# Whole 128-row products in place of packed 64-row halves for the filling work of an attention and Fourier-mixing kernel

## The chip, the cores and the metric

The kernel runs on one core of one Trainium2 chip. The metric is device time in microseconds (us) of one execution. The kernel before took 1701.76 us as the median of two runs (1701.06 to 1702.46).

## The reference

A token matrix `x` of 2048 x 512 goes through softmax attention with 32 heads of 16 columns, and another matrix through a two-sided Fourier product. A gate per token mixes the two:

```
q, k, v = split(x @ wqkv);  a = softmax(q k^T / 4) v @ wo          # 32 heads, 2048 x 2048 scores each
a2 = Bx @ Wd_re^T;  b2 = Bx @ Wd_im^T                               # 2048 x 512
b = Ws_re @ a2 - Ws_im @ b2                                         # 2048 x 2048 times 2048 x 512
g = sigmoid(sum(x * gate_w));  out = g * a + (1 - g) * b
```

The Fourier matrices come in as plain data. All operands are fp32. Products that must be exact to more than one rounded operand are made as three products of rounded parts: high by high, high by low, low by high.

## The kernel before, in words

**Stages.** A first part, up to about 600 us, makes q, k, v and both hidden-side Fourier products and most of the sequence-side product, and scans the scores for row maxima beside it. The second part is a loop of 512 steps, one per head pair `p` (16), half of the queries `h` (2) and block of 128 keys `kb` (16). A step makes scores (`qk`, line 232, operands `qs` and `ks` with 50 rows per head), takes their exponentials on ACT (`qk_both` and `qk_single`, lines 256 and 264) and adds values times exponentials (`pv`, line 825) into one PSUM bank `pvb`.

**Kinds of products.** TensorE's array has 128 rows. Three shapes of product meet in the loop:

- Score products take 50 rows, one head on rows 0 to 49 and the other on rows 64 to 113, so two of them run as a pair, one in each half of the rows. Their operands are fp32r (fp32 rounded for a single pass).
- Products of values take all 128 rows and 17 columns; four of them stand side by side in the columns (`tile_position=(0, r)`, with r in 0, 32, 64, 96). Their operands are fp32, and each shows as two records.
- Fourier and output products go through `halves_of` (line 203): the 128 rows of a product are cut into two products of 64 rows and 128 columns in fp32r, which run as a pair and write two PSUM banks `ps[0]` and `ps[1]`. Whoever reads the result adds the two banks.

**Filling.** Up to step 316 the loop also scans scores for the maxima of later pairs (line 157). From step `MIX` = 317 on no scan is left, and `outputs()` fills the steps instead: a generator, of which each step takes one piece by `next(fill)`. It runs through

- `spectral(t)` for two blocks of Fourier rows (one piece of 3 products per step, 16 steps each),
- `crosses()`: 14 groups of 24 products, 3 per step, over steps 349 to 460; `gather` (line 1099) reads each finished group, a copy of bank 0 and an addition of bank 1,
- from step `OUT` = 461 `mix_heads(t, steps)` for 16 blocks of output rows, 9 products each in two pieces of 4 and 5 (or four pieces of 2, 2, 2 and 3 for t = 0, 2 and 4); `take_in` (line 940) adds bank 0 and then bank 1 into the output tile `ys[t]`,
- `mix_some(t, (0, 1))` for six pairs of output blocks, one piece of 3 products per step and block group, by `mix_rest`.

Every group writes `pair_banks()`, a pair of PSUM banks of which there is one copy. The next group's first product waits until the readers of the group before have ended.

**What sets the order.** Nothing reorders the engines' queues: instructions run in the order in which Python writes them. In an even step the piece of filling comes first, then the scores; in an odd step it comes after the scores. Products of values of two steps are made together in the even steps, after the scores. So a period of two steps reads on TensorE: scores, products of values, scores, filling of the odd step and of the next even step.

Of the kernel before, what the change touches and what calls it, by code (L numbers as in the profile page):

```python
# [24 lines left out]
NB = S // P  # L25
# [25 lines left out]
MIX = TOTAL - FRONT + 1  # L51
OUT = MIX + NB * LATER - SAVED
# [16 lines left out]
def build(tc, xT, xr, wqkv, wo, wrT, wiT, cr, ci, ct, gate, out):  # L69
    nc = tc.nc  # L70
    with ExitStack() as ctx:
# [131 lines left out]
        def halves_of(ps, lhs, rhs, first, last):  # L203

            for j in range(2):
                r = slice(64 * j, 64 * j + 64)
                nc.tensor.matmul(ps[j], lhs[r], rhs[r], start=first, stop=last)  # L207

        def block(i):
            return big.tile([P, 512], F32R, tag=f"b{i}", name=f"b{i}")  # L210
# [62 lines left out]
        with ExitStack() as pf:  # L273
# [150 lines left out]
            with ExitStack() as px:  # L424
# [247 lines left out]
                for t in range(NB):  # L672
                    if 0 <= t - 2 < NB - 4:
                        after(32, split_operand, t - 2, load_operand(0, t - 2, rp), nc.gpsimd)
                    if t == 8:
                        first = stk.tile([P, 4, CS, P], F32, tag="stk", name="first")
# [10 lines left out]
            with ExitStack() as py:  # L687
# [38 lines left out]
                for n, (ph, t, u) in enumerate(coef):  # L726
# [41 lines left out]
                    for w in range(CS):  # L768
                        s = u * CS + w
# [9 lines left out]
                    if u == NU - 1:  # L779
                        tx = cp.tile([P, D], F32, tag="tx", name="tx")  # L780
                        last = n == len(coef) - 1
# [18 lines left out]
        with ExitStack() as pa:  # L800
# [63 lines left out]
            ys, oc = {}, {}  # L864
# [74 lines left out]
            def take_in(t, ps):  # L939
                nc.vector.scalar_tensor_tensor(ys[t], ps, g[:, t:t + 1], ys[t], op0=ALU.mult, op1=ALU.add)  # L940
# [20 lines left out]
            def spectral(t):  # L961

                ps = pair_banks()
                y = ap.tile([P, D], F32, tag="take", name="y", bufs=3)
                nc.sync.dma_start(y, y_d[t // 4][:, t % 4, :])
                for s in range(NB):
                    if s % CS == 0:
                        hi, lo = parts.pop(0)
                        load_unit()
                    if s % CS == 1:  # L970
                        split_unit()
                    w = s % CS
                    for i, (c_, a_) in enumerate(((hi, ah[s]), (hi, al[s]), (lo, ah[s]))):
                        halves_of((ps[:, 0, :], ps[:, 1, :]), c_[:, w, :], a_, s == 0 and i == 0, s == NB - 1 and i == 2)
                    if s < NB - 1:
                        yield
                for j in range(2):
                    nc.vector.scalar_tensor_tensor(y, ps[:, j, :], gm[:, t:t + 1], y, op0=ALU.mult, op1=ALU.add)
                nc.sync.dma_start(y_d[t // 4][:, t % 4, :], y)
                yield  # L980
# [117 lines left out]
            def gather(n, f, ps, r):  # L1098

                t = place(28 + f if n == 0 else 30 + f if n == 1 else None)  # L1100
                nc.vector.tensor_copy(t, ps[:, 0, :])
                nc.vector.tensor_add(t, ps[:, 1, :], t)
                add, sub = nc.gpsimd.tensor_add, nc.gpsimd.tensor_sub
                if n < 2:
                    tiles["nw"[n], f] = t
                if n == 1:
                    x = place()
                    add(x, tiles["n", f], t)
                    finish(r, (0, 1), f, x)
                elif n == 2:  # L1110
                    tiles["x", f] = t
                    sub(tiles["w", f], tiles["w", f], t)
                elif n == 3:
                    x = tiles["x", f]
                    add(x, x, t)
                    finish(r, (1, 0), f, x)
                    sub(tiles["n", f], tiles["n", f], t)
                elif n == 4:
                    sub(tiles["n", f], tiles["n", f], t)
                elif n == 5:  # L1120
                    sub(tiles["n", f], t, tiles["n", f])
                    finish(r, (0, 0), f, tiles["n", f])
                    add(tiles["w", f], tiles["w", f], t)
                elif n == 6:
                    add(tiles["w", f], tiles["w", f], t)
                    finish(r, (1, 1), f, tiles["w", f])

            def crosses():

                for n in range(len(CROSSES)):  # L1130
                    for f in range(2):
                        ps = pair_banks()
                        for u in range(8):
                            left, right = sets[f, u // CS], sets[None, u]
                            q = slice((u % CS) * P, (u % CS + 1) * P)
                            for i, (a, b) in enumerate(((0, 0), (0, 1), (1, 0))):
                                halves_of((ps[:, 0, :], ps[:, 1, :]), left[a][:, q], right[b],
                                          u == 0 and i == 0, u == 7 and i == 2)
                            if u < 7:
                                yield  # L1140
                        gather(n, f, ps, now[0] - HALVED)
                        yield
# [11 lines left out]
            def mix_heads(t, steps):  # L1154

                q = slice((t % 4) * P, (t % 4 + 1) * P)
                ps = pair_banks()
                n, last, ends = 0, 3 * (ND - 1), [sum(steps[:i + 1]) for i in range(len(steps))]
                assert ends[-1] == last
                for f in range(ND - 1):  # L1160
                    for a, b in ((0, 0), (0, 1), (1, 0)):
                        halves_of((ps[:, 0, :], ps[:, 1, :]), oc[t // 4, f, a][:, q], w2[f][b], n == 0, n == last - 1)
                        n += 1
                        if n in ends[:-1]:
                            yield
                for j in range(2):
                    take_in(t, ps[:, j, :])
                yield

            def mix_rest(t, ps, k, first, last):  # L1170
# [73 lines left out]
            for step in range(NP * PERIODS):  # L1244
                p, i = step // PERIODS, step % PERIODS
                h, kb = i // NB, i % NB
                now[0] = step
                if i == 18:
                    rows = load_use(p + 1, step >= MIX)
                if i >= 18:  # L1250
                    next(rows, None)
                if step in (MIX - 24, MIX - 20):
                    load_unit()
                if step in (MIX - 9, MIX - 7):
                    split_unit(int(step > MIX - 9))
                if OUT - 10 <= step < OUT - 4 or step >= OUT + 4:
                    next(operands, None)
                if step in (OUT - 8, OUT + 1):
                    output_rows(int(step > OUT))
                for n, at in enumerate((OUT - 25, (NP - 1) * PERIODS)):  # L1260
                    if at <= step < at + 8:
                        load_y(8 * n + step - at)
                if step >= MIX and step % 2 == 0:
                    next(fill)
                if step == 0:
                    pend.append((p, h, kb, ahead[:2]))
                    continue
                es = ahead[2:] if step == 1 else [qk2(p, h, kb, 0)]
                if step == 1:
                    es.append(qk2(p, h, kb, 1))  # L1270
                    flush()
                if late:
                    late.pop(0)()
                if step == 2:
                    es.append(qk2(p, h, kb, 1))
                if step > 1:
                    next_scan()
                if step > 2:
                    es.append(qk2(p, h, kb, 1))
                if step >= MIX and step % 2:  # L1280
                    next(fill)
                if step == NP * PERIODS - 1:
                    part(3, 0)
                done = None
                for _ in range(min(len(pend), 1) if step < MIX else 0 if step % 2 else 2):
                    done = flush()
                if done and done[2] == NB - 1:
                    halved.append((step + (10 if done[0] < NP - 2 else 7 if done[0] < NP - 1 else 3), quotients(*done[:2])))
                if halved and halved[0][0] <= step:
                    p_, h_ = halved[0][1][:2]  # L1290
                    divide(*halved.pop(0)[1])
                    if p_ == NP - 2:
                        output_rest(h_)
                    if p_ == NP - 2 + (h_ == 0):
                        output_last(h_)
                pend.append((p, h, kb, es))
                sum_quarters(step)
                crossing(step - HALVED)
                if TURNED <= step < TURNED + CROSS:
                    load_turned(NB - CROSS + step - TURNED)  # L1300
                if TURNED + 11 <= step < TURNED + 11 + CROSS:
                    take_turned(NB - CROSS + step - TURNED - 11)
# [77 lines left out]
```

## Time and profile before

| what | value |
|---|---|
| median of the runs | 1701.76 us |
| profiled execution | 1701.12 us |
| its span in the profile | 1699.3 us |
| TensorE (PE) busy | 1687.0 us, 13524 matmul records |
| weight loads (PEld) busy | 1039.9 us |
| ACT busy | 1491.1 us |
| DVE busy | 1185.7 us |
| POOL busy | 817.5 us |

The profiled execution took 1701.12 us, 1.8 us more than its span. PE and PEld are two rows of TensorE: the products and the loads of their stationary operands. A load that starts while a product still runs costs nothing by itself. A "busy" PE includes the time in which a product's results still leave the array, so that the starts of products tell more than their durations.

### The profile page before, as it was taken

To read this page: it belongs to the slowest core of one execution; us is meant where nothing else is said; L and a number is where in the kernel's file an instruction comes from. 1 tells how busy PE (TensorE), PEld (TensorE's weight loads), DVE (VectorE), ACT (ScalarE), POOL (GpSimd) and SP (SyncE) were. 2 spreads that over 40 slices of the span, in tenths; PEclk is the share of its full clock that TensorE was granted. 3 is DMA by queue.
4 is the path that set the end of the run, shared out by engine and by line. 5 is a ranking of instruction groups with operands and counts; after the bars stand their busy time and mean duration, and the time that the engine had idled before them with its cause. 6 is when DMAs were issued, how large, how long until landed. Compare 5 with 4: busy or idle time off the path is not lost.

```text
span 1699.3 us, 34660 instructions
## 1 busy us (share of the span) xinstructions
PE 1687.0 (99%) x13524; PEld 1039.9 (61%) x13524; DVE 1185.7 (70%) x1528; ACT 1491.1 (88%) x2468; POOL 817.5 (48%) x997
## 2 busy tenths in 40 slices
PE   9999999999999999999999999999999999999998
PEld 7889988999998784333333333333345555555554
DVE  5798888999989996666666676766733456563343
ACT  6447889888888888999999999999998888888886
POOL 4676876655556760444555364453323233334222
PEclk9999999999999999999999999999999999999999
DMA  7784668544448763455445455453526565575833
GB/s 274 265 270 99 218 217 241 153 129 122 120 125 210 207 133 71 122 128 123 134 119 133 101 130 137 96 144 56 111 56 147 148 148 146 136 192 135 196 92 128
DMA packets 151572, 251.08 MB, mean 148 GB/s; under 512 B 49792, under 2 KB 60528, under 8 KB 144112
## 3 DMA queue, kind: packets, MB, share of 16 engines
q1 hardware_dynamic: 136144, 227.49, 49.4%
q0 software_dynamic: 14688, 20.33, 5.1%
q8 instruction: 106, 1.74, 0.5%
q10 hardware_dynamic: 576, 1.05, 0.2%
q14 instruction: 58, 0.48, 0.1%
HBM read 168.56 MB, written 81.01 MB: 147 GB/s over the span
## 4 chain that ended last, share of the span: by engine, by line
PE 89%; DMA 4%; DVE 3%; POOL 2%; issue 1%; SPq 0%; ACT 0%; DVEq 0%; POOLq 0%; ACTq 0%
PE pvb L825 29%; PE xy L207 21%; PE s L232 19%; PE s L207 8%; PE s L178 8%; PE s L157 5%; DVE mx L159 3%; DMA qs<-q_d 1%; DMA early<-b_d 1%; DMA q_d<-eh 0%; DMA craw<-cr 0%; DMA raws<-xT 0%; POOL s L320 0%; DMA raws<-wqkv 0%; DMA abr<-b_d 0%
## 5 line engine op out<-in xcount | busy, mean ns | idle before, releaser
L256 ACT ACTIVATE eb<-s 128x1024 f32<-128x1024 f32 x512 | 582.5, 1138 | 58.1 <-PE s L232 58.1
L264 ACT ACTIVATE e<-s 128x512 f32<-128x512 f32 x1022 | 613.0, 716 | 0.0
L159 DVE TENSOR_REDUCE mx<-s 128x2 f32<-128x1024 f32 x380 | 461.5, 1225 | 193.1 <-PE s L157 192.7
L825 PE MATMUL pvb<-eb,va 128*17 128x512 f32 x2052 | 514.4, 597 | 0.3 <-DVE ob L834 0.3
L825 PE MATMUL pvb<-e,va 128*17 128x512 f32 x2044 | 513.5, 597 | 0.0
L183 DVE TENSOR_REDUCE mx<-s 128x1 f32<-128x512 f32 x644 | 434.6, 690 | 45.9 <-PE s L178 37.7
L232 PEld LDWEIGHTS s<-qs,ks 50*128 50x128 f32 x2048 | 215.7, 184 | 362.4 <-ACT eb L256 268.8
L181 ACT ACTIVATE s<-s 128x512 f32<-128x512 f32 x644 | 373.3, 586 | 72.8 <-PE s L178 42.4
L232 PE MATMUL s<-qs,ks 50*128 50x512 f32 x2048 | 424.6, 436 | 0.1
L207 PE MATMUL xy<-b,c 64*128 64x512 f32 x2448 | 395.1, 391 | 0.6 <-DVE s L320 0.3
L178 PE MATMUL s<-ks,qs 64*128 64x512 f32 x1288 | 305.5, 392 | 1.2 <-DVE mx L159 0.5
L207 PEld LDWEIGHTS xy<-b,c 64*128 64x128 f32 x2448 | 288.1, 184 | 22.7 <-DVE s L320 0.9
L825 PEld LDWEIGHTS pvb<-eb,va 128*17 128x17 f32 x2052 | 69.8, 96 | 187.9 <-issue 178.1
L178 PEld LDWEIGHTS s<-ks,qs 64*128 64x128 f32 x1288 | 165.4, 184 | 19.8 <-DVE mx L183 3.1
L157 PE MATMUL s<-ks,qs 48*128 48x512 f32 x760 | 166.6, 394 | 0.0
L844 POOL DMA_DIRECT2D r_d<-lc x31 | 18.0, 580 | 267.8 <-DVE lc L843 220.0
L207 PE MATMUL s<-b,b 64*128 64x512 f32 x1050 | 136.1, 390 | 0.4 <-DMA b<-o_d 0.4
L408 POOL TENSOR_TENSOR c<-craw,c 128x512 fp32r<-128x512 f32 x84 | 108.6, 1293 | 14.6 <-DVE c L407 8.0
L207 PE MATMUL xy<-w,b 64*128 64x512 f32 x768 | 115.3, 391 | 0.0
L837 POOL DMA_DIRECT2D lc<-ob x124 | 63.1, 515 | 108.0 <-DVE ob L834 103.9
L207 PEld LDWEIGHTS s<-b,b 64*128 64x128 f32 x1050 | 99.6, 185 | 24.0 <-issue 1.0
L846 POOL DMA_DIRECT2D rb<-r_d x124 | 60.5, 495 | 101.9 <-DMA r_d<-lc 97.9
(147 smaller groups left out, 1570.0 us busy)
## 6 DMA issues: line engine op xcount, KB each, us to landing
qs<-q_d SPq DMA_DIRECT2D x90, 256.0 KB
craw<-cr SPq DMA_DIRECT2D x60, 256.0 KB
craw<-ct SPq DMA_DIRECT2D x48, 256.0 KB
ks<-k_d SPq DMA_DIRECT2D x46, 256.0 KB
ks<-kf_d SPq DMA_DIRECT2D x44, 256.0 KB
kept_None<-sum SPq DMA_DIRECT2D x40, 256.0 KB
craw<-kept_None SPq DMA_DIRECT2D x40, 256.0 KB
craw<-ci SPq DMA_DIRECT2D x32, 256.0 KB
```

Source lines behind the costliest of these rows:

```text
L157: nc.tensor.matmul(ps[:, j, :], qs[b:b + 48, qb * P:(qb + 1) * P], ks[b:b + 48, c * 512:(c + 1) * 512], start=True, stop=True)
L159: nc.vector.tensor_reduce(mx[p][:, :, qb, c], ps, axis=AX.X, op=ALU.max)
L178: nc.tensor.matmul(ps, qs[b:b + 64, qb * P:(qb + 1) * P], ks[b:b + 64, c * 512:(c + 1) * 512], start=first, stop=True, skip_group_check=True)
L181: nc.scalar.activation(ps, ps, AF.Relu)
L183: nc.vector.tensor_reduce(mx[p][:, j, qb, c // 2:c // 2 + 1], ps, axis=AX.X, op=ALU.max)
L207: nc.tensor.matmul(ps[j], lhs[r], rhs[r], start=first, stop=last)
L232: nc.tensor.matmul(pss[j], ks[b:b + 50, kb * P:(kb + 1) * P], qs[b:b + 50, q0:q0 + 512], start=True, stop=True)
L256: nc.scalar.activation(e, ps, AF.Exp, scale=SCALE)
L264: nc.scalar.activation(e[j], pss[j], AF.Exp, scale=SCALE)
L408: sub(lo, raw, hi.bitcast(F32))
L825: nc.tensor.matmul(pvb[r:r + VC, :], va[:, kb, 2 * p + j, :], es[c][j], start=kb == 0, stop=kb == NB - 1, tile_position=(0, r))
L837: nc.gpsimd.dma_start(lc[32 * n:32 * n + 32, :], ob[r + DH:r + VC, :].rearrange("p (s e) -> p s e", e=16))
```

## The change

A second helper `whole_of` makes one product of 128 rows into one bank. The places that use it are `spectral`, `crosses` and `mix_heads`; their readers lose the addition of the second bank. `mix_some` and the last pieces keep `halves_of`. From step `OUT` on, the even step's piece of filling is taken after the products of values instead of before the scores; odd steps stay as they were.

```diff
+        def whole_of(ps, lhs, rhs, first, last):
+
+            nc.tensor.matmul(ps, lhs, rhs, start=first, stop=last)
+
@@ spectral @@
-                        halves_of((ps[:, 0, :], ps[:, 1, :]), c_[:, w, :], a_, s == 0 and i == 0, s == NB - 1 and i == 2)
+                        whole_of(ps[:, 0, :], c_[:, w, :], a_, s == 0 and i == 0, s == NB - 1 and i == 2)
...
-                for j in range(2):
+                for j in range(1):
                     nc.vector.scalar_tensor_tensor(y, ps[:, j, :], gm[:, t:t + 1], y, op0=ALU.mult, op1=ALU.add)
@@ gather @@
                 nc.vector.tensor_copy(t, ps[:, 0, :])
-                nc.vector.tensor_add(t, ps[:, 1, :], t)
@@ crosses @@
-                                halves_of((ps[:, 0, :], ps[:, 1, :]), left[a][:, q], right[b],
-                                          u == 0 and i == 0, u == 7 and i == 2)
+                                whole_of(ps[:, 0, :], left[a][:, q], right[b],
+                                         u == 0 and i == 0, u == 7 and i == 2)
@@ mix_heads @@
-                        halves_of((ps[:, 0, :], ps[:, 1, :]), oc[t // 4, f, a][:, q], w2[f][b], n == 0, n == last - 1)
+                        whole_of(ps[:, 0, :], oc[t // 4, f, a][:, q], w2[f][b], n == 0, n == last - 1)
...
-                for j in range(2):
-                    take_in(t, ps[:, j, :])
+                take_in(t, ps[:, 0, :])
@@ the loop of steps @@
-                if step >= MIX and step % 2 == 0:
+                if MIX <= step < OUT and step % 2 == 0:
                     next(fill)
...
                     if p_ == NP - 2 + (h_ == 0):
                         output_last(h_)
+                if step >= OUT and step % 2 == 0:
+                    next(fill)
                 pend.append((p, h, kb, es))
```

The order of TensorE's queue in a step pair of `crosses()`, before (score products L232, halves of a filling product L207, written `x2`):

```order
L232 MATMUL s_17896<-qs,ks 128x512 x2
L232 MATMUL s_17900<-qs,ks 128x512
L232 MATMUL s_17901<-qs,ks 128x512
L207 MATMUL s_17744<-b_17629,b_17730 128x512 x2
L207 MATMUL s_17744<-b_17630,b_17730 128x512 x2
L207 MATMUL s_17744<-b_17629,b_17731 128x512 x2
L207 MATMUL s_17744<-b_17651,b_17730 128x512 x2
L207 MATMUL s_17744<-b_17652,b_17730 128x512 x2
L207 MATMUL s_17744<-b_17651,b_17731 128x512 x2
L232 MATMUL s_17925<-qs,ks 128x512 x2
L232 MATMUL s_17929<-qs,ks 128x512
L232 MATMUL s_17930<-qs,ks 128x512
```

and now (score products L236, whole products L211):

```order
L236 MATMUL s_17755<-qs,ks 128x512 x2
L236 MATMUL s_17759<-qs,ks 128x512
L236 MATMUL s_17760<-qs,ks 128x512
L211 MATMUL s_17621<-b_17519,b_17607 128x512
L211 MATMUL s_17621<-b_17520,b_17607 128x512
L211 MATMUL s_17621<-b_17519,b_17608 128x512
L211 MATMUL s_17621<-b_17538,b_17607 128x512
L211 MATMUL s_17621<-b_17539,b_17607 128x512
L211 MATMUL s_17621<-b_17538,b_17608 128x512
L236 MATMUL s_17777<-qs,ks 128x512 x2
L236 MATMUL s_17781<-qs,ks 128x512
L236 MATMUL s_17782<-qs,ks 128x512
```

Six pairs of halves became six single products in the same place; the chunk still stands between two groups of scores.

The same queue in the output part, before: the end of the products of values (L825), the scores of the odd step, and the start of a group of `mix_heads`, nine pairs of which follow one another.

```order
L825 MATMUL pvb<-eb,va 17x512 x2
L825 MATMUL pvb<-e_0_9973,va 17x512
L825 MATMUL pvb<-e_0_9976,va 17x512
L232 MATMUL s_21183<-qs,ks 128x512 x2
L232 MATMUL s_21187<-qs,ks 128x512
L232 MATMUL s_21188<-qs,ks 128x512
L207 MATMUL s_21205<-b_20311,b_20924 128x512 x2
L207 MATMUL s_21205<-b_20312,b_20924 128x512 x2
L207 MATMUL s_21205<-b_20311,b_20926 128x512 x2
```

And now (products of values L829): the five whole products that end a group stand behind the products of values, and the next group begins after one set of scores.

```order
L829 MATMUL pvb<-e_0_9976,va 17x512
L211 MATMUL s_20620<-b_19900,b_20149 128x512
L211 MATMUL s_20620<-b_19899,b_20151 128x512
L211 MATMUL s_20620<-b_19903,b_20153 128x512
L211 MATMUL s_20620<-b_19904,b_20153 128x512
L211 MATMUL s_20620<-b_19903,b_20155 128x512
L236 MATMUL s_20655<-qs,ks 128x512 x2
L236 MATMUL s_20659<-qs,ks 128x512
L236 MATMUL s_20660<-qs,ks 128x512
L211 MATMUL s_20677<-b_19895,b_20436 128x512
L211 MATMUL s_20677<-b_19896,b_20436 128x512
```

Between the end of a group and the first product of the next (`s_20620` and `s_20677` are the same pair of banks) there were two sets of scores and the products of values; now there is one set of scores.

In `mix_some`, which keeps the halves, the second piece of a pair of output blocks moved in the same way. Now its place is:

```order
L829 MATMUL pvb<-e_2_9978,va 17x512
L207 MATMUL s_21044<-b_20225,b_20788 128x512 x2
L207 MATMUL s_21044<-b_20226,b_20788 128x512 x2
L207 MATMUL s_21044<-b_20225,b_20789 128x512 x2
L236 MATMUL s_21098<-qs,ks 128x512 x2
L236 MATMUL s_21102<-qs,ks 128x512
L236 MATMUL s_21103<-qs,ks 128x512
L207 MATMUL s_21108<-b_20220,b_20782 128x512 x2
L207 MATMUL s_21108<-b_20221,b_20782 128x512 x2
```

Here too one set of scores is left between the group that ends (`s_21044`) and the one that begins (`s_21108`).

Over the whole program the order of TensorE's queue has 576 whole products in place of 576 pairs, in 110 uninterrupted chunks: 72 of six products, and from step `OUT` on 19 behind scores (odd steps) and 19 behind products of values (even steps). DVE's queue has 32 instructions fewer: two in `spectral`, 14 in `gather`, 16 in `mix_heads`.

## The prediction

> **What bounds the kernel now.** I read the page first, then the stretches of the filled steps, then the chain of waits through two of them, and last single instructions around the places where TensorE changes from one kind of product to another. The page:
>
> ```profile
> PE 1687.0 (99%) x13524; PEld 1039.9 (61%) x13524; DVE 1185.7 (70%) x1528; ACT 1491.1 (88%) x2468; POOL 817.5 (48%) x997
> PEclk9999999999999999999999999999999999999999
> PE 89%; DMA 4%; DVE 3%; POOL 2%; issue 1%; SPq 0%; ACT 0%; DVEq 0%; POOLq 0%; ACTq 0%
> ```
>
> TensorE carries 89% of the chain that ends last, at full granted clock throughout. The stretches of the filled steps, the crossing part and the output part:
>
> ```profile
> core 0: us, PE busy (x) PEld busy (x) DVE busy (x) ACT busy (x) POOL busy (x), PEclk, DMA share, GB/s
> 1230.00:1560.00 330.00, 330.00 (x2702) 173.67 (x2700) 166.22 (x260) 296.14 (x458) 117.50 (x165) 1.00 0.54 135
> 1560.00:1690.00 130.00, 128.78 (x1040) 66.65 (x1039) 49.71 (x76) 105.52 (x162) 34.72 (x54) 1.00 0.53 139
> ```
>
> There TensorE has no gap, ACT is busy 90% and 81% of the time, DVE 50% and 38%. So time that the change adds to or takes from TensorE's queue is added to or taken from the end, and the saved DVE work lies beside TensorE and is worth nothing by itself. One period of two steps in the chain of waits (start, us, what):
>
> ```profile
> 1312.75 0.66 PE s L232 x4
> 1313.41 1.39 PE s L207 x12
> 1314.80 0.49 PE s L232 x4
> 1315.29 1.84 PE pvb L825 x16
> 1317.13 0.66 PE s L232 x4
> ```
>
> Six pairs of halves take 1.39 us, 0.23 each. The same four score products (two pairs) take 0.49 behind the filling and 0.66 behind the products of values. What happens there shows in the starts of single instructions (PEld is the load of a stationary operand):
>
> ```profile
> 1332.38 0.41 PE L232 MATMUL s<-qs,ks 50*128 50x512 f32 x2
> 1332.72 0.61 PE L825 MATMUL pvb<-eb,va 128*17 128x512 f32 x2
> ...
> 1333.59 0.60 PE L825 MATMUL pvb<-eb,va 128*17 128x512 f32 x2
> 1334.02 0.60 PE L825 MATMUL pvb<-eb,va 128*17 128x512 f32 x2
> 1334.56 0.50 PE L232 MATMUL s<-qs,ks 50*128 50x512 f32 x2
> ...
> 1334.89 0.40 PE L232 MATMUL s<-qs,ks 50*128 50x512 f32 x2
> 1334.90 0.19 PEld L207 LDWEIGHTS s<-b,b 64*128 64x128 f32 x2
> 1335.13 0.40 PE L207 MATMUL s<-b,b 64*128 64x512 f32 x2
> ```
>
> From scores to filling (both pairs of 64-row halves of the array) nothing is lost: the load at 1334.90 starts with the scores' second pair, and the filling follows 0.24 after that pair. From scores to products of values the step is 0.34 in place of 0.23: 0.11 lost. From values to scores it is 0.54 where one group follows the other after 0.43: 0.11 lost. And behind that the first score pair takes 0.33 until the second starts, in place of 0.23, since its 128-column load did not run ahead: 0.10 more. So a **change of shape** costs 0.11 for emptying the array, plus 0.10 where a load of 128 columns follows.
>
> **The change, part by part.** First, what whole products add. Before, the filling shared its shape with the scores, and a chunk had no boundary of its own. Now each chunk between two sets of scores has two: scores to whole products, whole products to scores. The order counts 72 such chunks in the spectral and crossing parts and 19 in the odd steps of the output part: 182 new boundaries. (The 19 chunks behind products of values end in a boundary to the scores that the products of values had before.) The trace of before has no whole product in fp32r, but it has whole 128 x 128 products at the end of the program, the transposes:
>
> ```profile
> 1685.13 0.39 PE L207 MATMUL s<-b,b 64*128 64x512 f32 x2
> 1685.46 0.33 PE L1318 MATMUL s<-ident,ob 128*128 128x128 f32 x1
> 1685.62 0.38 PE L1318 MATMUL s<-ident,ob 128*128 128x128 f32 x2
> ...
> 1687.47 0.27 PE L1327 MATMUL s<-ident,rb 128*128 128x128 f32 x1
> 1687.68 0.50 PE L207 MATMUL s<-b,b 64*128 64x512 f32 x1
> 1687.68 0.49 PE L207 MATMUL pvb<-b,b 64*128 64x512 f32 x1
> 1688.01 0.39 PE L207 MATMUL s<-b,b 64*128 64x512 f32 x1
> ```
>
> Halves to whole: 0.33 in place of 0.23. Whole to halves, with nothing to wait for: 0.21 behind a transpose, while two transposes that follow without a gap stand 0.11 apart (the row of 1685.62: 0.38 for two, of which the second takes 0.27); then 0.33 to the next pair. That is the same 0.10 and 0.10. The price of a boundary is bounded below by 0 (if these rows show a change of number format, see the first rival), above by 0.22; I take 0.21, from the rows that change between the very shapes in question. 182 x 0.21 = **38.2 us**. Nothing hides it, as TensorE has no gap in these stretches.
>
> The Trainium skill, in "TensorEngine Tiling (Array Packing)", section Key Properties, says that changing the tiling mode, not just the tile, drains the engine. The trace agrees, with 0.11 at each such place; by that rule the 182 boundaries are all paid for, which is the sum above.
>
> Second, the 19 changes from products of values (four column tiles of 17) to whole products. No row shows this change. Below it costs 0, if the shared 128 rows are what counts; above 0.22. I take 0.21 since the tiling differs as it does between the other shapes: **4.0 us**.
>
> Third, what a whole product saves. A pair of halves costs 0.23. The nearest row for 128 rows is the products of values: 16 records in 1.84 less 0.11 of boundary are 8 passes of 512 columns, 0.216 each. A whole product lies between 0.216 and 0.23; I take 0.22, so 576 x 0.01 = **5.8 us** saved (bounds 0 and 8).
>
> Fourth, the waits for the one pair of banks. Before, between the last product of a group in the output part and the first of the next stood scores, products of values, scores. Now it is one set of scores, because the chunk of the even step moved behind the products of values. The readers on DVE:
>
> ```profile
> L940 DVE SCALAR_TENSOR_TENSOR y<-s,g,y 128x512 f32<-128x512 f32 x49 | 35.9, 749 | 70.5 <-PE s L207 69.9
> 1655.67 0.40 PE L207 MATMUL s<-b,b 64*128 64x512 f32 x2
> 1656.14 1.41 DVE L940 SCALAR_TENSOR_TENSOR y<-s,g,y 128x512 f32<-128x512 f32 x2 [2.66 <-PE s L207]
> ```
>
> The first reader starts 0.47 after a group's last pair starts; one reading takes 0.75, two take 1.41. I estimate 0.06 until TensorE is released. In `mix_heads` one reading is left, so the banks are free 1.28 after the last product's start. TensorE wants them after two boundaries and two score pairs: 0.33 + 0.33 + 0.33 = 0.99. It waits 0.29, at 16 group ends: **4.6 us**. In `mix_some` both readings stay: free after 1.94, wanted after three pair steps of 0.23 = 0.69, so 1.25 plus 0.10 for the late load, at 6 group ends (the last hands the banks to `part(3, 0)`): **8.1 us**. Queued behind such a wait on TensorE are the scores of the next step, so ACT falls idle and DVE too; ACT has 10 to 19% to spare there. In the crossing part the readers have two sets of scores and the products of values as before, and finish 0.69 earlier, which frees nothing that TensorE waits for: 0.
>
> Sum: 38.2 + 4.0 - 5.8 + 4.6 + 8.1 = 49.1 us. The profiled execution took 1701.1, so **1750 us**, 2.9% more; its time lies 0.6 us below the median of the runs, which does not matter here. The sum's own range is 1738 (19 changes free, boundaries at 0.18, readers a little quicker) to 1760 (boundaries at 0.225, TensorE gaining nothing by whole products).
>
> **The rivals.** *The array empties only when the number format changes.* Everywhere in the trace where 0.11 is lost, one side is fp32 (products of values, transposes) and the other fp32r. Scores, halves and whole products are all fp32r. If the format is the mechanism, the 182 boundaries cost nothing, and the chunks behind products of values only take over the boundary that the scores had there. Then 5.8 us are saved, and the bank waits grow, as TensorE reaches the banks sooner: in `mix_heads` after 0.69, so it waits 0.59 + 0.10 at 16 ends, 11.0 us, with 8.1 in `mix_some`. 1701.1 - 5.8 + 11.0 + 8.1 = 1714, which is no change that a measurement of this kernel can tell (about 2% is), and not slower by it. From a boundary price of about 0.15 on the time goes over 2%. For it: the confounding is complete. Against it: the array's rows and columns are cut differently at each of those places too, and a product's record, 0.39 long where the next starts after 0.23, says that its results are still on their way through rows that a differently cut product needs. That is an argument and no measurement, so the rival keeps a fair chance.
>
> *The array empties, but the load runs ahead.* Half the price at the boundaries: 182 x 0.11 = 20.0, 2.1 for the 19, waits between (6 + 8.1), so 1701.1 + 20.0 + 2.1 - 5.8 + 14.1 = 1732. Against it: behind every boundary of the trace the first pair takes 0.33.
>
> *A whole product cannot load while another runs.* With all rows taken, each of the 466 whole products that is not first in its chunk would show its load, 0.10: 47 us more, 1797. Against it:
>
> ```profile
> 1685.46 0.55 PE L1318 MATMUL s<-ident,ob 128*128 128x128 f32 x3
> 1685.63 0.24 PEld L1318 LDWEIGHTS s<-ident,ob 128*128 128x128 f32 x2
> ```
>
> Loads of 128 rows and 128 columns start at 1685.63 while transposes of the same rows run. The Trainium skill, in "TensorE: Matmul & The Clock Gate", Part 3 ("What overlaps and what doesn't"), states that a load overlaps with products in flight only when the row group differs. These rows, and the loads at 1334.90 under score products of the same rows, differ from it; the measurement decides.
>
> *The boundaries cost nothing and the banks are read in time* (the readers' 1.28 and 1.94 being hidden by something that I do not see): 1701.1 - 5.8 = 1695, within 2% as well.
>
> **How the numbers follow.** My forecast (every boundary at about 0.21) has 0.68; the format rival 0.17; load ahead 0.08; no overlap of loads 0.04; nothing paid 0.03. Predicted 1750. The range goes from 1712, so that the format rival's sum lies inside, to 1762; the forecast alone would be 1738 to 1760. Slower by over 2% means over 1736: forecast and the third rival but for a small part, 0.70. Within 2%: the format rival, load ahead, nothing paid, and that small part, 0.28. Faster by over 2% is 0.02, for what I do not see.
>
> **What would show each step.** In the profile after, the period of the crossing part grows from 4.38 to about 4.75 us; the starts around a chunk stand 0.34 apart at both its ends, and the first product of a chunk is followed by the second after 0.32 to 0.33, the others after 0.22. Behind products of values the first whole product comes 0.54 after the last group. In the output part TensorE shows idle time before the first product of a group, released by DVE, of about 0.3 us 16 times and 1.3 us 6 times. DVE loses some 22 us of busy time, 32 readings of about 0.7. The time up to step 316 stays as it is. If the starts at a chunk's ends stand 0.23 apart, the format rival is right and my main term is gone; if whole products stand over 0.3 apart, the third one is.

## The result

The changed kernel takes 1752.29 us (1752.27 to 1752.31, two runs) against 1701.76: a ratio of 1.030, with a 95% interval of 1.025 to 1.034. It is slower by 50.5 us. The profiled execution has a span of 1750.3 us against 1699.3. The prediction was 1750 us, 1712 to 1762.

The profile's page of the changed kernel, the same rows as before:

```profile
PE 1727.3 (99%) x12948; PEld 1011.5 (58%) x12948; DVE 1164.9 (67%) x1496; ACT 1499.3 (86%) x2468; POOL 818.9 (47%) x997
PEclk9999999999999999999999999999999999999999
PE 90%; DVE 4%; DMA 2%; POOL 1%; issue 1%; ACT 0%; SPq 0%; DVEq 0%; POOLq 0%
```

There are 576 matmul records fewer, and 32 DVE instructions and 20.8 us of DVE's time fewer. The granted clock is the same, and the longer time is on TensorE's row. DVE's share of the chain that ends last grew from 3% to 4%.

The chain of waits through one period of the crossing part (start, us, what):

```profile
1314.28 0.66 PE s L236 x4
1314.95 1.57 PE s L211 x6
1316.52 0.66 PE s L236 x4
1317.18 1.84 PE pvb L829 x16
1319.02 0.66 PE s L236 x4
```

The period is 4.74 us (1314.28 to 1319.02) in place of 4.38. The products of values take 1.84 as before. Six whole products take 1.57 where six pairs of halves took 1.39, and the scores behind the filling now take 0.66, as those behind products of values always did, in place of 0.49. Single starts around one chunk, and the loads (PEld) behind its first boundary:

```profile
1333.51 0.40 PE L236 MATMUL s<-qs,ks 50*128 50x512 f32 x2
1333.84 0.50 PE L211 MATMUL s<-b,b 128*128 128x512 f32 x1
...
1334.17 0.62 PE L211 MATMUL s<-b,b 128*128 128x512 f32 x2
...
1335.09 0.39 PE L211 MATMUL s<-b,b 128*128 128x512 f32 x1
1335.41 0.50 PE L236 MATMUL s<-qs,ks 50*128 50x512 f32 x2
...
1333.84 0.30 PEld L211 LDWEIGHTS s<-b,b 128*128 128x128 f32 x2 [0.37 <-issue]
1334.17 0.19 PEld L211 LDWEIGHTS s<-b,b 128*128 128x128 f32 x1
```

Scores to whole: 0.33 in place of 0.23. First to second whole product: 0.33. The row of 1334.17 holds two products, 0.62 long with the last taking 0.39, so they start 0.23 apart. Whole to scores: 0.32. So both ends of a chunk pay, though scores and whole products are both fp32r. That alone rules out the format rival. The loads show the second half of the price. The row of 1333.84 holds two loads, 0.30 long; one load takes 0.19, so the second begins 0.11 after the first product, and the second whole product comes 0.10 late. The third load starts together with the second product (1334.17), and from there on the products stand 0.23 apart.

In the output part, a group of the heads and then one of the last groups (products of values, whole products, scores and the wait for the banks):

```profile
1620.18 0.60 PE L829 MATMUL pvb<-eb,va 128*17 128x512 f32 x2
1620.72 1.43 PE L211 MATMUL s<-b,b 128*128 128x512 f32 x5
1622.08 0.73 PE L236 MATMUL s<-qs,ks 50*128 50x512 f32 x4
1623.00 0.73 PE L211 MATMUL s<-b,b 128*128 128x512 f32 x2 [0.18 <-DVE y L944]
...
1708.14 0.63 PE L236 MATMUL s<-qs,ks 50*128 50x512 f32 x4
1709.81 0.97 PE L207 MATMUL s<-b,b 64*128 64x512 f32 x6 [1.04 <-DVE y L944]
```

From the last products of values to the first whole product 0.54, as it was from products of values to scores: the 19 new changes of that sort are paid too. Before the next group TensorE shows 0.18 us of idle time in the heads' groups and 1.04 in the last ones, which keep two readings. In sum over the filled steps (engine and line, waited for, us in total, times, longest; one of the seven waits of L207 is the 0.2 behind the last group of the heads):

```profile
PE s L207 <- DVE y L944: 6.5, 7, 1.1
PE s L211 <- DVE y L944: 2.8, 15, 0.2
```

By the starts of the scores of steps 317, 349, 461 and 499 in both traces, the 51.0 us of span came so: 0.8 before step 317 (where nothing was changed; that part differs by -0.4 to 0.8 in the other kernels too), 5.8 in the spectral part (16 chunks), 20.9 in the crossing part (56 chunks), 15.8 in the groups of the heads, 6.6 in the last groups up to step 511 and 1.1 behind them.

### The profile page after: what moved, and what is told of

It reads as the page before. It is cut to its first block, busy times and chain, and to the rows that moved or that the text cites. A ratio compares the mean times of both kernels' runs of the same rounds, so it can differ in the third digit from the quotient of the medians.

```text
span 1750.3 us, 33478 instructions
## 1 busy us (share of the span) xinstructions
PE 1727.3 (99%) x12948; PEld 1011.5 (58%) x12948; DVE 1164.9 (67%) x1496; ACT 1499.3 (86%) x2468; POOL 818.9 (47%) x997
## 4 chain that ended last, share of the span: by engine, by line
PE 90%; DVE 4%; DMA 2%; POOL 1%; issue 1%; ACT 0%; SPq 0%; DVEq 0%; POOLq 0%
PE pvb L829 28%; PE xy L207 21%; PE s L236 19%; PE s L211 9%; PE s L178 8%; PE s L157 4%; DVE mx L159 3%; DVE y L944 1%; PE s L207 1%; DMA early<-b_d 0%; POOL c L412 0%; DMA craw<-cr 0%; DMA raws<-wqkv 0%; POOL s L324 0%; DMA abr<-b_d 0%
## 5 line engine op out<-in xcount | busy, mean ns | idle before, releaser
L829 PE MATMUL pvb<-eb,va 128*17 128x512 f32 x2052 | 514.4, 597 | 0.3 <-DVE ob L838 0.3
L829 PE MATMUL pvb<-e,va 128*17 128x512 f32 x2044 | 513.4, 597 | 0.0
L236 PE MATMUL s<-qs,ks 50*128 50x512 f32 x2048 | 431.1, 443 | 1.0 <-ACT eb L260 0.9
L236 PEld LDWEIGHTS s<-qs,ks 50*128 50x128 f32 x2048 | 196.6, 184 | 374.3 <-ACT eb L260 269.0
L207 PE MATMUL xy<-b,c 64*128 64x512 f32 x2448 | 395.5, 391 | 0.4 <-ACT s L324 0.3
L178 PE MATMUL s<-ks,qs 64*128 64x512 f32 x1288 | 310.1, 392 | 1.2 <-DVE mx L159 0.5
L207 PEld LDWEIGHTS xy<-b,c 64*128 64x128 f32 x2448 | 290.9, 184 | 22.9 <-ACT s L324 0.7
L829 PEld LDWEIGHTS pvb<-eb,va 128*17 128x17 f32 x2052 | 69.9, 96 | 198.5 <-issue 190.9
L211 PE MATMUL s<-b,b 128*128 128x512 f32 x480 | 136.2, 414 | 2.8 <-DVE y L944 2.8
L211 PEld LDWEIGHTS s<-b,b 128*128 128x128 f32 x480 | 82.8, 188 | 60.3 <-issue 31.9
L207 PE MATMUL xy<-w,b 64*128 64x512 f32 x768 | 116.0, 391 | 0.0
```

The costliest lines, as they stand in the source:

```text
L178: nc.tensor.matmul(ps, qs[b:b + 64, qb * P:(qb + 1) * P], ks[b:b + 64, c * 512:(c + 1) * 512], start=first, stop=True, skip_group_check=True)
L211: nc.tensor.matmul(ps, lhs, rhs, start=first, stop=last)
L236: nc.tensor.matmul(pss[j], ks[b:b + 50, kb * P:(kb + 1) * P], qs[b:b + 50, q0:q0 + 512], start=True, stop=True)
L829: nc.tensor.matmul(pvb[r:r + VC, :], va[:, kb, 2 * p + j, :], es[c][j], start=kb == 0, stop=kb == NB - 1, tile_position=(0, r))
```

## The experiments

The "cut" below is the way in which the array is divided into tiles: two of 64 rows (scores and halves), four of 32 columns (products of values) or one whole. The theory: TensorE's array empties at each change of cut, and the loads just behind it do not run ahead; together about 0.2 us a change in this kernel, whatever is computed. Beside it stand waits for the one pair of banks, caused by the move. Each run is compared with the kernel before as measured beside it (1700.75 to 1701.42 us). The rivals: the format of the operands empties the array; whole products are slow in themselves; the loss is mainly the move's.

**Whole products without the move.**

```diff
-                if MIX <= step < OUT and step % 2 == 0:
+                if step >= MIX and step % 2 == 0:
                     next(fill)
...
-                if step >= OUT and step % 2 == 0:
-                    next(fill)
```

> Whole products as in the change, but the even step's piece of filling stays before the scores from the first filled step to the last; nothing else differs. If each change of the array's cut costs about 0.20 us: 91 chunks between scores have two boundaries each, at 0.37 us a chunk as the crossing part of the changed kernel showed (4.74 us a period in place of 4.375), so 1701.8 + 91 x 0.37 = 1735.5 us, 1733 to 1739. If the loss comes mainly from the move in the output part (waits for the one pair of banks): near 1702, 1700 to 1708.

Measured 1734.14 us, a ratio to the kernel before of 1.0196 (1.0181 to 1.0212). The 72 chunks of the first parts cost 26.7 us as in the changed kernel. In the output part the period now reads, in the chain of waits:

```profile
1635.23 0.66 PE s L236 x4
1635.89 1.84 PE pvb L829 x16
1637.74 0.66 PE s L236 x4
1638.40 2.29 PE s L211 x9
1640.68 0.66 PE s L236 x4
```

That is 5.45 us (1635.23 to 1640.68), where the kernel before has 5.06, and no wait for DVE's readings. The output part, steps 461 to 498, lost 5.6 us in its 19 chunks, 0.30 each and not 0.37: the 13 chunks of nine products lost 0.40, three of five products 0.14, and three of four nothing. Whole products by themselves make two thirds of the loss; the move makes the remaining 17 to 18 us.

**The move without whole products.**

```diff
-                if step >= MIX and step % 2 == 0:
+                if MIX <= step < OUT and step % 2 == 0:
                     next(fill)
...
+                if step >= OUT and step % 2 == 0:
+                    next(fill)
```

> The move alone: halves everywhere as before, the even step's piece behind the products of values from the output part on. If only changes of cut cost something: their number is the same as before, so 1702 us. If the wait for the pair of banks costs what the sum said: with halves there are two readings at every group end (1.94 us until the banks are free, wanted after 0.69, plus 0.10 for the late load), 1.35 us at 16 ends of the heads' groups and at 6 of the later ones, 29.7 us, so 1731 us, 1724 to 1736.

Measured 1733.01 us, 1.0190 (1.0175 to 1.0206), with everything up to step 461 as before. Its waits of TensorE:

```profile
PE s L207 <- DVE y L940: 24.9, 22, 1.2
PE s L232 <- ACT eb L256: 1.7, 4, 0.4
```

There are 22 waits, at the ends of 16 + 6 groups, as counted, of 1.13 us each as idle time. Idle time counts only from the end of the last score pair, 0.39 after its start, where the next product would have started 0.23 after it; so a wait delays by 0.16 more, and by 0.10 for the late load behind it (the second pair follows after 0.33 to 0.34). That is 1.39 a wait, 30.6 of the 31.2 us by which the span grew. So the move has a price of its own in the waits, with no change of cut added. In the changed kernel the single bank halves the reading and so takes most of it away again; what it costs there is a change of cut instead.

**The move only for the groups of the heads.**

```diff
-                if MIX <= step < OUT and step % 2 == 0:
+                if (MIX <= step < OUT or step >= OUT + 38) and step % 2 == 0:
                     next(fill)
...
-                if step >= OUT and step % 2 == 0:
+                if OUT <= step < OUT + 38 and step % 2 == 0:
                     next(fill)
```

> The change, but the last 12 steps, whose products are halves, take the even step's piece before the scores again. If the six long waits for the pair of banks (6.5 us by DVE in the changed kernel's trace, plus 0.10 each for the late load) set that part: 1752.3 - 7 = 1745 us. If they are covered by something else: 1752 us.

Measured 1744.58 us, 1.0259 (1.0241 to 1.0276). That is 7.7 us under the changed kernel, 6.7 when each is set against the kernel before beside it; by the starts the part from step 499 on is 6.8 us shorter. This is the price of the six long waits.

**The move from the first filled step on.**

```diff
-                if MIX <= step < OUT and step % 2 == 0:
-                    next(fill)
...
-                if step >= OUT and step % 2 == 0:
+                if step >= MIX and step % 2 == 0:
                     next(fill)
```

> Whole products, and the even step's piece goes behind the products of values from the first filled step on: the 72 chunks of six become 144 chunks of three, which adds 72 changes from products of values to whole products (0.22 each by the changed kernel's trace) and no other. If the count of changes sets the time: 1752.3 + 15.6 = 1768 us, and up to 1785 if the shorter stretch between two sets of scores also makes TensorE wait for ACT (0.2 us in 72 periods) and for the banks at 16 more group ends (0.2 each). If the array does not empty between products of values and whole products: 1752 or less.

Measured 1788.93 us, 1.0521 (1.0505 to 1.0536): slower yet, a little above the upper end that was given. The chain of waits:

```profile
1400.58 0.66 PE s L236 x4
1401.24 0.89 PE s L211 x3
1402.14 0.98 PE s L236 x4
1403.11 1.84 PE pvb L829 x16
1404.95 0.89 PE s L211 x3
1405.85 0.66 PE s L236 x4
```

and the load of the last score product in the 0.98:

```profile
1402.62 0.18 PEld L236 LDWEIGHTS s<-qs,ks 50*128 50x128 f32 x1 [0.20 <-ACT e L268]
```

The scores behind the short chunk take 0.98 in place of 0.66: 0.3 us a period, where 0.2 was expected. The row shows the last score product waiting for ACT's exponential `e` of the step before: between the two sets of scores stand three products in place of six, too few for ACT to empty the scores' banks. So the 36.6 us over the changed kernel (37.4 in the spectral and crossing parts by the starts) are about 72 x 0.21 = 15 us of changes of cut and about 72 x 0.3 = 22 us of this wait, the larger of the two.

**Whole products in the spectral and crossing parts alone.** The change, with halves back in `mix_heads` and the move undone as in the first run (not shown in the cut).

```diff
-                        whole_of(ps[:, 0, :], oc[t // 4, f, a][:, q], w2[f][b], n == 0, n == last - 1)
+                        halves_of((ps[:, 0, :], ps[:, 1, :]), oc[t // 4, f, a][:, q], w2[f][b], n == 0, n == last - 1)
...
-                take_in(t, ps[:, 0, :])
+                for j in range(2):
+                    take_in(t, ps[:, j, :])
```

> Whole products in the spectral and crossing parts alone, halves in the output part, no move. If each chunk between scores costs 0.37 us: 1701.8 + 72 x 0.37 = 1728.4 us, and the output part (step 461 to the end) takes what it took before, 137.1 us. If the loss per chunk depends on what follows in the output part: something else by more than 3 us.

Measured 1728.04 us (one run, against 1701.42 beside it, also one run): 26.6 us, 0.37 per chunk. The part from step 461 to the end takes 136.6 us, before 137.1. The parts add up.

**One whole product in each chunk of halves.** In `crosses` of the kernel before; both banks are read as before.

```diff
+                                if u % 2 == 1 and i == 0:
+                                    whole_of(ps[:, 0, :], left[a][:, q], right[b], False, u == 7 and i == 2)
+                                else:
                                     halves_of((ps[:, 0, :], ps[:, 1, :]), left[a][:, q], right[b],
                                               u == 0 and i == 0, u == 7 and i == 2)
```

> The kernel before, with one whole product in the middle of each chunk of six in the crossing part (it adds into bank 0; the other five stay halves, and both banks are read as before): 56 whole products, 112 changes of cut. If the price is per change, at 0.187 each as in the crossing part of the changed kernel (20.9 us for 112): 1701.8 + 20.9 = 1722 us, the crossing part (steps 349 to 460) 266 us in place of 245, as with six whole products in every chunk. If whole products are slow in themselves (20.9 us over 336 of them, 0.062 each): 1701.8 + 3.5 = 1705 us.

Measured 1723.27 us, 1.0130 (1.0115 to 1.0145). The chain of waits through a chunk:

```profile
1412.66 0.66 PE s L236 x4
1413.33 0.70 PE s L207 x6
1414.03 0.43 PE s L211
1414.46 0.67 PE s L207 x4
1415.13 0.47 PE s L236 x4
```

One whole product among halves loses as much as six in a row: 21.9 us over 112 changes, 0.195 each. It takes 0.43 in place of 0.23, and the two pairs behind it 0.67 in place of 0.46; the scores behind the chunk, whose neighbours are halves again, are back at 0.47.

**Every second product whole.** The same with another condition.

```diff
-                                if u % 2 == 1 and i == 0:
+                                if (3 * u + i) % 2 == 1 and 3 * u + i < 23:
```

> The same with every second product of the crossing groups whole (but for each group's last): 154 whole products, fewer than the changed kernel's 336 there, but six changes of cut in three chunks of a group and four in the fourth, 308 in all. If the price is per change: 308 x 0.187 = 57.6, 1759 us, more than the changed kernel. If it is per whole product: 154 x 0.062 = 9.5, 1711 us.

Measured 1762.06 us, 1.0358 (1.0340 to 1.0375).

```profile
1410.53 0.67 PE s L236 x4
1411.20 0.23 PE s L207 x2
1411.43 0.43 PE s L211
1411.87 0.43 PE s L207 x2
1412.30 0.43 PE s L211
1412.73 0.43 PE s L207 x2
1413.16 0.42 PE s L211
1413.59 0.66 PE s L236 x4
```

Each product that follows another cut takes 0.43, whichever cut it has. 60.7 us over 308 changes are 0.197 each, the same as over 112. With fewer whole products than the changed kernel, this one loses more in the crossing part (305.1 us, against 266.0 and 245.1 before). The price is per change of cut; whole products in themselves cost about what a pair costs.

**Another format with the same cut.** The spectral halves of the kernel before, read as fp32.

```diff
-                        halves_of((ps[:, 0, :], ps[:, 1, :]), c_[:, w, :], a_, s == 0 and i == 0, s == NB - 1 and i == 2)
+                        halves_of((ps[:, 0, :], ps[:, 1, :]), c_[:, w, :].bitcast(F32), a_.bitcast(F32), s == 0 and i == 0, s == NB - 1 and i == 2)
```

> The kernel before, with the 96 pairs of halves of the two spectral blocks read as fp32 in place of fp32r: the format changes between scores and filling, the cut of the array does not. (Parts of the operands that fp32r would round are kept, so the sums differ in the last digits.) Each such pair takes four passes, 0.86 us in place of 0.23 as the products of values do, 60 us more in 16 periods of two steps. If only the cut empties the array: the first half of a chunk starts 0.23 to 0.24 us after the scores' second pair, and the scores 0.86 after the last pair, about 1762 us. If the format empties it as well: 0.33 and 0.97, and a first pair that takes 0.10 more, about 1769 us.

Measured 1761.83 us (one run, against 1701.42 beside it, also one run).

```profile
1269.58 1.84 PE pvb L825 x16
1271.42 0.67 PE s L232 x4
1272.09 5.15 PE s L207 x24
1277.24 0.46 PE s L232 x4
1277.70 1.84 PE pvb L825 x16
...
1271.69 0.40 PE L232 MATMUL s<-qs,ks 50*128 50x512 f32 x2
1271.93 0.59 PE L207 MATMUL s<-b,chi 64*128 64x512 f32 x2
```

The first fp32 pair starts 0.24 after the scores' second pair, the chunk is 12 x 0.43 long, and the scores behind it take 0.46, no more than behind fp32r halves (0.49). The 16 chunks are each 3.76 us longer (5.15 in place of 1.39), 60.2 us; the run is 60.4 longer, which leaves next to nothing for its 32 changes of format. With the changed kernel's starts (a change of cut at the same format, which costs) this separates the two.

## Why the prediction was right

**The main term.** 182 new boundaries at 0.21 less the gain of the products were put at 38.2 - 5.8 = 32.4 us. The two first parts lost 26.7 us in 72 chunks, 0.37 a chunk or 0.186 a boundary. The 19 chunks of the output part, in the run where they stand between scores without the move, lost 5.6: together 32.3. The mechanism, emptying plus a late load, stands as the steps put it: 0.33 and 0.33 at the beginning of a chunk, 0.32 and 0.34 at its end. That the two sums meet so closely is luck, because three sizes were off: a boundary was put too dear, the products gained nothing, and six chunks of the output part did not pay in full.

The last of these goes against "Nothing hides it". In the kernel before, a period of the output part with four pairs of filling lasts 4.37 us, as long as one with six (4.38), because the scores behind the short chunk wait for ACT:

```profile
1577.57 0.98 PE L232 MATMUL s<-qs,ks 50*128 50x512 f32 x4
1578.06 0.18 PEld L232 LDWEIGHTS s<-qs,ks 50*128 50x128 f32 x1 [0.19 <-ACT e L264]
```

Four score products take 0.98 there in place of 0.65, as the load of the last one waits for ACT's exponential. So a boundary that delays the scores costs nothing or part of its price.

**The gain by whole products** was not there. I put 0.22 for one, from the passes of the products of values, and 5.8 us in all. Averaged over the crossing part, whole products inside a chunk start 0.231 apart and pairs of halves 0.228. The four starts at the two ends of a chunk are together 0.38 longer than before, so a boundary costs 0.19 and not 0.21; and the products of values start 0.017 sooner behind the scores (0.327 in place of 0.343), which brings the chunk to 0.37.

**The 19 changes to whole products behind products of values**: 0.21 was assumed with no row for it. The first whole product comes 0.54 after the last products of values, where one group of these follows another after 0.43, and the second whole product after 0.34 in place of 0.23. That is about 0.21, 4.0 us, as put.

**The waits for the banks**: 4.6 us were put for the groups of the heads. The first product of the next group starts 0.58 after the last score pair in place of 0.33, 0.25 at each of 16 ends and so about 4 us; the idle time of 0.18 is smaller, since it counts only from the end of the score pair. For the six last groups the sum had 8.1, where the run without their waits gained 6.7 to 7.7.

**What the sum did not have** is ACT: behind the short chunks of two products the scores wait for a bank that ACT still reads (0.9 us of idle time in four places of the changed kernel). It is little here, but it is also what hid boundaries in the run without the move, and it came to 22 us in the run with the move from the first filled step on.

Of the rivals, the format fell by the starts and by the run in fp32. That the load runs ahead behind a change fell by the rows of 1333.84. Loads under products of the same rows did run ahead elsewhere: the load at 1334.17 starts with a whole product, and whole products stand 0.23 apart, not 0.33. The Trainium skill, in "TensorE: Matmul & The Clock Gate", Part 3 ("What overlaps and what doesn't"), states that a load overlaps with products in flight only when the row group differs. These rows do not bear that out. The Trainium skill, in "TensorEngine Tiling (Array Packing)", Key Properties, states that changing the tiling mode drains the engine. The trace agrees, and puts 0.09 to 0.11 us on it, besides the load.

Nothing in the runs points to a faster version than the kernel before: its halves share the cut of the scores, so its filling adds no change of cut, and a whole product is no faster than a pair.

## What to carry to other kernels

Count the changes of cut in TensorE's queue, not the instructions: in this kernel a product that had the same cut as its neighbours added nothing to its own time, and one that differed cost about 0.2 us at each side, unless something else, here ACT, already held the queue at that place. Two half products as a pair can be the better form of one whole product if what stands around them is cut in halves. When work moves between two groups that share one PSUM tile, add up what the reader needs against what is left between the groups, and ask what else used that stretch (here ACT's exponentials). All of this was measured with 512 columns a product, at full granted clock; other sizes were not tried.

## What the runs showed of the hardware that was not expected

A change between fp32 and fp32r operands at the same cut cost no time that the starts show (0.24 at the first fp32 pair, and 0.46 for the scores behind the last). A whole fp32r product of 128 rows and 512 columns and a pair of 64-row halves have the same spacing, 0.23 us. The same pairs in fp32 show as two records each, and the records ran 0.43 apart, a little under twice 0.23; why was not tried.

A load runs late not only behind a change of cut: behind the waits for the banks in the run with the move alone, where halves follow scores of the same cut, the second pair also started 0.33 to 0.34 after the first in place of 0.23.
